# Another table for the attention unit of a four-layer kernel: three shared maxima in place of four, other value phases, GpSimd's jobs at other steps, one store of the maxima

## The chip, the cores and the metric

The kernel runs on one core of a Trainium2 chip. The metric is the device time of one execution in microseconds (us); a time is the median of several runs. The engines are named as in the profile: PE is the matrix engine, PEld its loads of weights, DVE the vector engine, ACT the scalar engine, POOL is GpSimd, SP issues DMAs. A "q" behind an engine's name is its queue.

## What is computed

Four attention layers with residuals on x of 2048 tokens by 576, 32 heads of 18 elements, all in float32: A, B, A, B. Layer A has a key and a value for each head, layer B one key and one value for all heads.

```python
def _A_ref(x, wqkv, wo):
    ...
    q, k, v = qkv[0], qkv[1], qkv[2]
    scores = jnp.einsum("bhqd,bhkd->bhqk", q, k) * (Dh ** -0.5)
    p = _softmax(scores, axis=-1)
    o = jnp.einsum("bhqk,bhkd->bhqd", p, v)
    return (lambda x, *d: x.transpose(*d))(o, 0, 2, 1, 3).reshape(B, S, D) @ wo
...
x = A_x
x = x + _A_ref(_layernorm(x, axis=-1), A_wqkv, A_wo)
x = x + _B_ref(_layernorm(x, axis=-1), B_wq, B_wk, B_wv, B_wo)
x = x + _A_ref(_layernorm(x, axis=-1), A_wqkv, A_wo)
x = x + _B_ref(_layernorm(x, axis=-1), B_wq, B_wk, B_wv, B_wo)
```

## The kernel before

**Work of a layer.** After layernorm and the projections, the heads are taken in 16 pairs; of a pair, head half a = 0 lies on partitions 0 to 63 and a = 1 on 64 to 127, so that a tile of either half uses half of PE's rows. For each pair p and each block u of 512 queries there are three kinds of PE work:

- *m tiles* (lines 590 and 601): scores of 128 queries against 512 keys, 32 tiles for one (p, u). DVE takes each row's maximum (line 606, into `mx`). The maxima are needed as rows of the q operand of the next kind, so they run LEAD = 14 steps ahead of it.
- *e tiles* (line 823): scores of 128 keys against 512 queries with the maxima already subtracted, 32 for one (p, u). ACT takes the exponential (line 827, into a buffer `pt`).
- *value columns* (line 865): `pt` times the values, summed over all keys in the bank `oacc`. They run PV_LAG = 928 columns behind.

Some m tiles are of kind r (line 590): the tile is a difference of two key blocks' scores. ACT takes its relu (line 599) into one buffer named `relu`, which all of them share; some tiles later DVE adds that buffer to the other block's scores and takes the row maximum in one fused instruction (line 604, with a short read of the accumulator behind it). So one DVE instruction serves two tiles, and this is what "shared maximum" means.

**Order.** It is written out by hand in the table UNIT and repeats with a period of 10 phases, called a unit here: 32 m and r tiles, 32 e tiles and 4096 value columns. A phase is a list of tiles and then a number of value columns. A tile is written as kind, head half, rank: `r10` is an r tile of half 1 with rank 0. A step is 4 e tiles, and a unit is 8 steps. Each engine executes its instructions in program order.

**Banks.** m and e tiles share seven PSUM banks. They are kept in a list by last use; a tile with rank 0 takes the bank that was used longest ago, with rank 1 the one after that, and so on. Before PE may write a bank, the ACT or DVE instruction that reads its earlier tile must be done. This is the loop, and the choice of a bank:

```python
def oldest(rank=0):
    return lambda name: bank(lru[rank], name)
...
rows, cols = UNIT[phase % len(UNIT)]
run_todo(LEAD + sum(e_next) / 4)
for kind, a, rank in rows:
    if kind == "e":
        exp_next(a, rank)
    elif m_done[0] < 4 * ns:
        max_mm(oldest(rank))
...
pv_cols(cols - skip)
```

**Jobs at steps.** What is not in the table is given a step with `at` and is emitted by `run_todo` at the start of the first phase that reaches it. For a block (p, u): two POOL instructions turn the maxima into `hl` (`max_final`, lines 797 to 801, emitted two m tiles after the block's last); at NM_AT DVE transposes them and SP stores them to `m_d` (`max_store`, lines 806 and 808); at ROW_AT SP loads them as rows of q (`max_rows`, line 812); at SUM_AT and later steps POOL and SP do the sums, the reciprocals and the output (`o_sum`, `l_part`, `l_inv`, `l_out`, `l_rows`, `o_mul`, `o_out`). Weights of `wo` and of the next layer come in chunks c = 0 to 4 during the attention: SP loads a chunk into `raw` (`load_wsm`, `load_a`, `load_b`; lines 192 to 195), and `finish_loads` lets POOL split it into a high and a low part (lines 176 and 205).

Of the kernel before, what the change touches and what calls it, by code (L numbers as in the profile page):

```python
# [8 lines left out]
F32 = mybir.dt.float32  # L9
# [9 lines left out]
P = 128  # L19
NCH = S // P  # L20
NPAIR = H // 2
# [24 lines left out]
STEPS = 8  # L46
LEAD = 14
NM_AT = 2.5
ROW_AT = 5
SUM_AT = 3  # L50
L_AT = 5
INV_AT = 8
R_AT = 8
# [8 lines left out]

UNIT = [("e00 m10 m02 e10 e01 e10 m00", 448),
# [9 lines left out]
UNIT = [([(o[0], int(o[1]), int(o[2])) for o in rows.split()], cols) for rows, cols in UNIT]  # L75
PV_LAG = 928
UNIT_M = [(kind, a) for rows, _ in UNIT for kind, a, _ in rows if kind != "e"]
assert len(UNIT_M) == 32 and sum(cols for _, cols in UNIT) == 4096


@with_exitstack
def tile_kernel(ctx: ExitStack, tc: tile.TileContext, A_x, A_wqkv, A_wo, B_x, B_wq, B_wk, B_wv, B_wo, out):
    nc = tc.nc
# [6 lines left out]
    dram = ctx.enter_context(tc.tile_pool(name="dram", bufs=1, space=DRAM))  # L90
# [42 lines left out]
    kd_d = dram.tile([2 * DH, 3, 512], F32, name="kd_d")  # L133


    m_d = [dram.tile([2, 2, 4, P], F32, name=f"m_d{i}") for i in range(4)]
    o_d = dram.tile([D, S], F32, name="o_d")
    r_d = dram.tile([H, S], F32, name="r_d")

# [271 lines left out]
    for layer in range(4):  # L411
        is_a = layer % 2 == 0
# [79 lines left out]
        def q_slot(p):  # L492
            return (3, 5, 1)[p % 3] if is_a else (3, 4, 0)[p % 3]
# [173 lines left out]
        def max_pairs():  # L667

            if is_a:
                run_todo(m_done[0] // 4)  # L670
            elif m_done[0] == 44:
                max_store(0, 0)
            elif m_done[0] == 48:
                max_rows(0, 0)
            for i in range(4):
                max_mm(etile if i == 3 else mtile)
            while m_full:
                max_final(*m_full.pop()[0])
# [124 lines left out]
        def max_store(p, u):  # L803

            tr = pool.tile([P, 32], F32, name="tr")
            nc.vector.transpose(tr, nms.pop((p, u)).bitcast(F32))
            for b in range(4):
                nc.sync.dma_start(m_d[u].rearrange("j a q (b i) -> b (j a q) i", b=4)[b], tr[32 * b:32 * b + 16, :])

        def max_rows(p, u):  # L810
            for a in range(2):
                nc.sync.dma_start(big_f[64 * a + KM:64 * a + KE, q_slot(p), u * 512:(u + 1) * 512],
                                  m_d[u][:, a].rearrange("j q p -> j (q p)"))

        def exp_mm(p, u, i, rank):

# [97 lines left out]
        relu, raw = (pool.tile([P, 640], F32, tag="xh", bufs=2, name=n) for n in ("relu", "raw"))  # L914
        todo = {}

        def at(b, f, *args):
            todo.setdefault(b, []).append((f, args))

        for p in range(NPAIR):  # L920
            for u in range(4):
                b = STEPS * (4 * p + u) + STEPS - 1
                if is_a or p or u:
                    at(b + NM_AT, max_store, p, u)
                    at(b + ROW_AT, max_rows, p, u)
                for d, f in ((SUM_AT, o_sum), (L_AT, l_part), (INV_AT, l_inv), (R_AT, l_out), (RB_AT, l_rows),
                             (MUL_AT, o_mul), (O_AT, o_out)):
                    at(b + LEAD + d, f, p, u)
            if p + 1 < NPAIR and is_a:
                for d, f in ((0, diff_in), (3, diff_split), (5, diff_out), (10 if p else 8, diff_rows)):  # L930
                    at(max(LEAD, 32 * p - 8) + d, f, p + 1)
            if is_a and p in (0, 1):
                at(LEAD + 20 + 32 * p, load_rows, q_slot(p + 1), 2 * (p + 1) * DH, DH, 1536, S)
            if p + 1 < NPAIR:
                for i in range(4 if is_a else 2):
                    at(LEAD + 32 * (p - 1) + 1 + 8 * i if p else LEAD + 1 + 4 * i, load_part, p + 1, i)
        for c in range(5):
            at(49 + 4 * c, finish_loads)
            at(48 + 4 * c, load_wsm, c, A_wo if is_a else B_wo, nc.gpsimd, nc.gpsimd, False,
               (raw[:, :288], raw[:, 288:]))  # L940
            if layer < 3:
                b = LEAD + 32 * (NPAIR - 1) + 2 * c
                load = load_b if is_a else load_a
                at(b - 29, finish_loads)
                at(b + 3, finish_loads)
                at(b - 30, load, c, (2,), nc.gpsimd, nc.gpsimd, raw)
                at(b + 2, load, c, (0,), nc.gpsimd, nc.gpsimd, raw)

        def run_todo(st):
            for n in sorted(n for n in todo if n <= st):  # L950
                for f, args in todo.pop(n):
                    f(*args)

        b = LEAD + ns
# [19 lines left out]
        while m_done[0] < 4 * ns:  # L974
            rows, cols = UNIT[phase % len(UNIT)]
            run_todo(LEAD + sum(e_next) / 4)
# [56 lines left out]
```

## Time and profile before

| | |
|---|---|
| median of 3 runs | 5553.27 us (5551.57 to 5559.15) |
| the profiled execution | 5554.74 us |
| its span, first to last instruction | 5553.0 us |
| ACT exponentials, L827 | 8192, busy 4182.4 us |
| DVE row maxima, L606 | 6208, busy 3959.1 us |
| DVE fused maxima, L604 | 992, busy 686.1 us |
| ACT relus, L599 | 992, busy 622.2 us |

The page gives each engine's busy time and its share of the span, then the chain of work that ended last, then groups of instructions by line with their number and mean length. Busy times of ACT and DVE count from an instruction's start to its end, and instructions that follow each other closely overlap by some tenths of a us; how fast an engine really goes is read from the distance of starts in the timeline.

### The profile page before, as it was taken

How to read it: one execution, taken by the hardware profiler on the slowest of the kernel's cores; microseconds unless marked ns; L12 is line 12 of the kernel's file. 1: busy time of each engine (PE TensorE's matmuls, PEld its weight loads, DVE VectorE, ACT ScalarE, POOL GpSimd, SP SyncE). 2: the span in 40 equal slices, each digit the busy share in tenths (PEclk: the TensorE clock that was granted, in tenths of full speed). 3: DMA queues.
4: the chain of work that ended last, by engine and by line, in shares of the span. 5: the costliest groups of instructions: out<-in, count | busy, mean ns of one | idle time of the engine just before them, and what ended most of it. 6: DMA issues, size and time to landing. Idle time of an engine off the chain costs nothing.

```text
span 5553.0 us, 143953 instructions
## 1 busy us (share of the span) xinstructions
PE 5519.8 (99%) x55774; PEld 3110.0 (56%) x55774; DVE 4949.8 (89%) x9489; ACT 4883.1 (88%) x9872; POOL 1836.8 (33%) x2396
## 2 busy tenths in 40 slices
PE   9999999999999999999999999999999999999999
PEld 8655555554855555555686555555548555555556
DVE  4699999998699999999647999999977999999995
ACT  2599999999389999999725999999992999999996
POOL 3143333334233333333412433333342333333332
PEclk9999999999999999999999999999999999999999
DMA  6421111111421101001243211111114211110102
GB/s 199 133 55 47 43 47 42 47 44 24 132 70 24 24 21 24 21 23 25 61 168 111 59 44 46 43 46 45 42 31 137 59 24 24 24 24 21 24 14 81
DMA packets 275188, 301.69 MB, mean 54 GB/s; under 512 B 135246, under 2 KB 193190, under 8 KB 265214
## 3 DMA queue, kind: packets, MB, share of 16 engines
q1 hardware_dynamic: 274502, 292.49, 19.0%
q8 instruction: 437, 7.16, 0.6%
q14 instruction: 249, 2.04, 0.1%
HBM read 168.50 MB, written 119.86 MB: 52 GB/s over the span
## 4 chain that ended last, share of the span: by engine, by line
PE 96%; POOL 1%; issue 1%; DMA 1%; DVE 0%; SPq 0%; ACT 0%; POOLq 0%; ACTq 0%; DVEq 0%
PE oacc L865 37%; PE pse L823 27%; PE psm L601 17%; PE psn L259 7%; PE psq L433 5%; PE psm L590 3%; PE ps L251 0%; DMA big<-qk_d 0%; POOL ev L445 0%; ACT pt L827 0%; DVE mx L606 0%; DMA xo<-in_A_x_dram 0%; DMA raw<-in_B_wk_dram 0%; DMA xx<-qk_d 0%; DMA big<-m_d 0%
## 5 line engine op out<-in xcount | busy, mean ns | idle before, releaser
L827 ACT ACTIVATE pt<-pse 128x512 f32<-128x512 f32 x8192 | 4182.4, 614 | 23.1 <-PE pse L823 11.7
L606 DVE TENSOR_REDUCE mx<-psm 128x1 f32<-128x512 f32 x6208 | 3959.1, 685 | 119.8 <-PE psm L601 77.2
L823 PE MATMUL pse<-big 64*128 64x512 f32 x8192 | 2288.2, 433 | 3.2 <-DMA big<-m_d 1.9
L601 PE MATMUL psm<-big 62*128 62x512 f32 x7200 | 2194.9, 443 | 7.9 <-DVE mx L604 4.3
L823 PEld LDWEIGHTS pse<-big 64*128 64x128 f32 x8192 | 1177.1, 185 | 1071.6 <-ACT pt L827 742.3
L865 PE MATMUL oacc<-pt,vbuf 128*19 128x32 f32 (+11 forms) x26544 | 1731.6, 368 | 4.0 <-DVE oc L176 4.0
L601 PEld LDWEIGHTS psm<-big 62*128 62x128 f32 x7200 | 913.1, 184 | 172.7 <-ACT pt L827 33.9
L865 PEld LDWEIGHTS oacc<-pt,vbuf 128*19 128x19 f32 x26544 | 534.6, 98 | 826.2 <-issue 664.4
L176 POOL TENSOR_SCALAR os<-oc 32x512 f32<-32x512 f32 x512 | 313.2, 612 | 1917.2 <-ACT oc L874 1508.9
L893 POOL TENSOR_TENSOR rl<-lt,mone 128x8 f32<-128x8 f32 x256 | 423.1, 1653 | 984.4 <-DMA lt<-os 933.5
L604 DVE CUSTOM_DVE_ANT_0 relu<-psm,relu 128x512 f32<-128x512 f32 x992 | 686.1, 692 | 32.6 <-PE pse L823 1.1
L599 ACT ACTIVATE relu<-psm 128x512 f32<-128x512 f32 x992 | 622.2, 627 | 0.2
L865 PE MATMUL oacc<-pt,vy 128*19 128x288 f32 (+3 forms) x8176 | 567.2, 383 | 0.0
L441 ACT ACTIVATE ev<-psq 128x512 fp32r<-128x512 f32 (+1 forms) x112 | 66.9, 598 | 327.7 <-PE psq L433 226.2
L906 POOL TENSOR_TENSOR os<-os,rb 96x512 f32<-96x512 f32 x256 | 327.7, 1280 | 26.4 <-DMA rb<-r_d 25.3
L884 POOL TENSOR_TENSOR os<-os,oc 96x512 f32<-96x512 f32 x256 | 327.9, 1281 | 21.3
L865 PEld LDWEIGHTS oacc<-pt,vy 128*19 128x19 f32 x8176 | 190.2, 98 | 239.5 <-issue 196.0
L259 PE MATMUL psn<-wsm,xx 128*128 128x288 f32 x2240 | 307.9, 296 | 0.7 <-ACT pt L827 0.7
L259 PEld LDWEIGHTS psn<-wsm,xx 128*128 128x128 f32 x2240 | 298.6, 188 | 13.7 <-issue 11.7
L447 DVE TENSOR_TENSOR ev<-psq,ev 128x512 fp32r<-128x512 f32 (+1 forms) x84 | 58.0, 691 | 214.1 <-ACT ev L441 195.1
L590 PE MATMUL psm<-big 54*128 54x512 f32 x512 | 215.1, 420 | 0.0
L590 PE MATMUL psm<-xx,big 54*128 54x512 f32 x480 | 201.2, 419 | 0.0
(93 smaller groups left out, 2368.3 us busy)
## 6 DMA issues: line engine op xcount, KB each, us to landing
big<-qk_d SPq DMA_DIRECT2D x172, 432.0 KB
qk_d<-ev SPq DMA_DIRECT2D x96, 512.0 KB
qk_d<-ev SPq DMA_DIRECT2D x120, 256.0 KB
rb<-r_d SPq DMA_DIRECT2D x512, 36.0 KB
o_d<-os SPq DMA_DIRECT2D x512, 36.0 KB
m_d<-tr SPq DMA_DIRECT2D x1024, 2.0 KB
o<-o_d SPq DMA_DIRECT2D x64, 256.0 KB
xx<-qk_d SPq DMA_DIRECT2D x120, 72.0 KB
```

The costliest lines, as they stand in the source:

```text
L259: nc.tensor.matmul(ps, lhs[:, xc, :], wsm[:, wc, h * 288:(h + 1) * 288], start=i == 0, stop=i == len(TERMS) - 1)
L590: nc.tensor.matmul(ps.rearrange("p (h t) -> p h t", h=2) if p == 0 or not is_a else ps, q[b:b + 3 * DH, c0:c0 + P], k, start=True, stop=True)
L599: nc.scalar.activation(t, ps, AF.Relu)
L601: nc.tensor.matmul(ps, q[b:b + KM, c0:c0 + P], k[b:b + KM, kb * 512:(kb + 1) * 512], start=True, stop=True)
L604: nc.vector.tensor_tensor_reduce(t, ps, t, 1.0, LOWEST, OP.add, OP.max, mx[:, r:r + 1])
L606: nc.vector.reduce_max(mx[:, r:r + 1], ps, axis=AX.X)
L823: nc.tensor.matmul(e, k[r:r + KE, kc * P:(kc + 1) * P], q[r:r + KE, u * 512:(u + 1) * 512], start=True, stop=True)
L827: nc.scalar.activation(pt, e, AF.Exp, scale=SCALE)
L865: nc.tensor.matmul(oacc[j:j + DH + 1, cs], v_of(kc)[:, 2 * p + a if is_a else 0, :], pts[p, u, i][:, cs], start=kc < 2 and c0 == 0, stop=k ...
L884: nc.gpsimd.tensor_tensor(t[:96], t[:96], oc[:96], op=OP.add)
L893: nc.gpsimd.tensor_tensor(rl, lts.pop((p, u)), mone, op=OP.pow)
L906: nc.gpsimd.tensor_tensor(t[:96], t[:96], rb[:96], op=OP.mult)
```

## The change

The table UNIT is replaced. Four r tiles a unit become three, so one more of the 32 tiles goes to DVE alone. The phases hold 6 or 7 tiles (before 4 to 7) and 352 to 480 value columns (before 256 to 480). SUM_AT moves `o_sum` by 0.75 of a step. The loads of `wo` move by 2 steps. The loads of the next layer's weights come 4 steps apart (before 2 steps) and each is finished one step after it was started. The transposed maxima are stored with one DMA of all 128 partitions to a larger `m_d` (before four DMAs of 16 partitions each); `max_rows` reads the same values.

```diff
-SUM_AT = 3
+SUM_AT = 3.75
...
-        ("e10 e01 r10 m00", 256),
...
-        ("m10 e00 m12 m00 e11 e01 e10", 448),
-        ("e01 m10 e02 e10 r01 m11 m00", 416),
...
+        ("m00 e10 e01 m10 m11 r00", 448),
+        ("e00 m10 e00 m01 e10 m01 e10", 416),
...
-    m_d = [dram.tile([2, 2, 4, P], F32, name=f"m_d{i}") for i in range(4)]
+    m_d = [dram.tile([4, 2, 4, P], F32, name=f"m_d{i}") for i in range(4)]
...
-            for b in range(4):
-                nc.sync.dma_start(m_d[u].rearrange("j a q (b i) -> b (j a q) i", b=4)[b], tr[32 * b:32 * b + 16, :])
+            nc.sync.dma_start(m_d[u].rearrange("j a q (b i) -> b (j a q) i", b=4), tr)
...
-                                  m_d[u][:, a].rearrange("j q p -> j (q p)"))
+                                  m_d[u][:2, a].rearrange("j q p -> j (q p)"))
...
-            at(49 + 4 * c, finish_loads)
-            at(48 + 4 * c, load_wsm, c, A_wo if is_a else B_wo, nc.gpsimd, nc.gpsimd, False,
+            at(51 + 4 * c, finish_loads)
+            at(50 + 4 * c, load_wsm, c, A_wo if is_a else B_wo, nc.gpsimd, nc.gpsimd, False,
...
-                b = LEAD + 32 * (NPAIR - 1) + 2 * c
+                b = STEPS * 4 * (NPAIR - 1) + 4 * c - 14
...
-                at(b - 29, finish_loads)
-                at(b + 3, finish_loads)
-                at(b - 30, load, c, (2,), nc.gpsimd, nc.gpsimd, raw)
-                at(b + 2, load, c, (0,), nc.gpsimd, nc.gpsimd, raw)
+                at(b + 1, finish_loads)
+                at(b + 33, finish_loads)
+                at(b, load, c, (2,), nc.gpsimd, nc.gpsimd, raw)
+                at(b + 32, load, c, (0,), nc.gpsimd, nc.gpsimd, raw)
```

One line fewer stands ahead of `max_rows`, so lines behind it have a number smaller by one in the changed kernel: the exponential is L826 there, the e tile L822, the value columns L864.

**First place: ACT and DVE, in the middle of a unit.** ACT in the kernel before, from the r tile of the fourth phase on (in brackets the engines or DMA queues whose signal an instruction waits for):

```order
L599 ACTIVATE relu<-psm 128x512 [waits DVE_49,PE_49]
L827 ACTIVATE pt<-pse 128x512 [waits PE_49] x2
L599 ACTIVATE relu<-psm 128x512 [waits PE_49,Activation_49]
L827 ACTIVATE pt<-pse 128x512 [waits PE_49] x7
L599 ACTIVATE relu<-psm 128x512 [waits DVE_49,PE_49]
```

And in the changed kernel, from the r tile of the fifth phase on:

```order
L599 ACTIVATE relu<-psm 128x512 [waits DVE_49,PE_49]
L826 ACTIVATE pt<-pse 128x512 [waits PE_49] x3
L599 ACTIVATE relu<-psm 128x512 [waits DVE_49,PE_49]
L826 ACTIVATE pt<-pse 128x512 [waits PE_49,Activation_49]
L826 ACTIVATE pt<-pse 128x512 [waits PE_49] x7
```

DVE from the transpose at the start of the sixth phase on, before (the two rows of line 604, called ISA here, are the fused maximum and the read of its accumulator):

```order
L806 STREAM_TRANSPOSE tr<-hl_115 128x32 [waits DMAHW2_49,DMAHW1_49,DMAHW7_49,DMAHW0_49,Pool_49]
L604 ISA relu,mx_89<-psm,relu 128x512 [waits PE_49,Activation_49]
L604 ISA mx_89 128x1
L606 TENSOR_REDUCE mx_89<-psm 128x1 [waits PE_49] x2
L604 ISA relu,mx_89<-psm,relu 128x512 [waits PE_49]
```

And in the changed kernel:

```order
L806 STREAM_TRANSPOSE tr<-hl_114 128x32 [waits DMAHW4_49,Pool_49]
L606 TENSOR_REDUCE mx_90<-psm 128x1 [waits PE_49] x2
L604 ISA relu,mx_90<-psm,relu 128x512 [waits PE_49,Activation_49]
L604 ISA mx_90 128x1
L606 TENSOR_REDUCE mx_90<-psm 128x1 [waits PE_49] x3
```

In the changed kernel the sixth phase's tiles for DVE are m00, m10 and m11, and m11 is served by the fused instruction, which reads the relu of r12 (fifth phase). The signal of DVE that the relu of r00 waits for is the one of this fused instruction. In the kernel before, the relu of r01 (seventh phase) waits for the fused instruction of that phase's m10, its first tile for DVE.

**Second place: PE, end of the sixth phase and the seventh.** The changed kernel from m11 on (rows of L601, L590: m and r tiles; L822: e tiles; L864: value columns):

```order
L601 MATMUL psm<-big 128x512 [waits DVE_49]
L590 MATMUL psm<-big 128x512 [waits Activation_49]
L864 MATMUL oacc<-pt,vbuf 19x384 x4
L864 MATMUL oacc<-pt,vbuf 19x64 [waits Activation_49]
L864 MATMUL oacc<-pt,vbuf 19x64 x3
L822 MATMUL pse<-big 128x512
L601 MATMUL psm<-big 128x512 [waits DVE_49]
L822 MATMUL pse<-big 128x512
L601 MATMUL psm<-big 128x512 [waits DVE_49]
L822 MATMUL pse<-big 128x512 [waits Activation_49]
L601 MATMUL psm<-big 128x512 [waits Activation_49]
L822 MATMUL pse<-big 128x512 [waits DVE_49]
```

The kernel before, its sixth phase's value columns and its seventh phase:

```order
L865 MATMUL oacc<-pt,vbuf 19x448 x4
L823 MATMUL pse<-big 128x512 [waits Activation_49]
L601 MATMUL psm<-big 128x512 [waits DVE_49]
L823 MATMUL pse<-big 128x512 [waits Activation_49]
L823 MATMUL pse<-big 128x512 [waits DVE_49]
L590 MATMUL psm<-xx,big 128x512 [waits Activation_49]
L601 MATMUL psm<-big 128x512 [waits Activation_49]
L601 MATMUL psm<-big 128x512 [waits DVE_49]
L865 MATMUL oacc<-pt,vbuf 19x32 x4
```

In the changed kernel the L601 row that waits for ACT, the seventh phase's second m01, is the tile that takes the bank of r00; the last row's e10 takes the bank of m11.

**Third place: POOL, at the load of the next layer's weights near the end of layer 0.** Before (raw is the loaded chunk, os the sums, hl the maxima):

```order
L188 MEMSET raw 128x256
L176 TENSOR_SCALAR big<-raw 128x2x128
L205 TENSOR_TENSOR big<-raw,big 128x2x128
L176 TENSOR_SCALAR os_112<-oc 32x512 x2
L884 TENSOR_TENSOR os_112<-os_112,oc 96x512
L188 MEMSET raw 128x256
L176 TENSOR_SCALAR hl_114<-neg 128x8
L801 TENSOR_TENSOR hl_114<-neg,hl_114 128x8
```

And in the changed kernel:

```order
L188 MEMSET raw 128x256
L176 TENSOR_SCALAR big<-raw 128x2x128
L205 TENSOR_TENSOR big<-raw,big 128x2x128
L176 TENSOR_SCALAR hl_115<-neg 128x8
L801 TENSOR_TENSOR hl_115<-neg,hl_115 128x8
L176 TENSOR_SCALAR os_113<-oc 32x512 x2
L883 TENSOR_TENSOR os_113<-os_113,oc 96x512
L905 TENSOR_TENSOR os_112<-os_112,rb 96x512
```

The two instructions of `hl` stood behind `o_sum` and now stand ahead of it.

More of the change, by code (lines that the diff above doesn't have):

```diff
@@ L60 @@
 TAIL = 2
-UNIT = [("e00 m10 m02 e10 e01 e10 m00", 448),
[9 rows of a table removed]
+UNIT = [("m10 e00 e00 m10 m01 e10", 448),
[9 rows of a table added]
 UNIT = [([(o[0], int(o[1]), int(o[2])) for o in rows.split()], cols) for rows, cols in UNIT]
```

13 rows, old and new, of the table UNIT are left out of this document.

## The prediction

> **What bounds the kernel now.** The page's first and fourth parts come first: which engine is busy, and which engine the chain that ended last runs through.
>
> ```profile
> span 5553.0 us, 143953 instructions
> PE 5519.8 (99%) x55774; PEld 3110.0 (56%) x55774; DVE 4949.8 (89%) x9489; ACT 4883.1 (88%) x9872; POOL 1836.8 (33%) x2396
> ...
> PE 96%; POOL 1%; issue 1%; DMA 1%; DVE 0%; SPq 0%; ACT 0%; POOLq 0%; ACTq 0%; DVEq 0%
> ```
>
> PE is the path, and ACT and DVE stand a little below it. The view by stretches says how regular this is: layer 0 from its second unit on, and one unit (ten phases) of layer 1.
>
> ```profile
> 239.80:1231.50 991.70, 991.70 (x10804) 509.94 (x10801) 965.70 (x1837) 990.51 (x1999) 368.54 (x469) 1.00 0.19 49
> 2010.50:2028.86 18.36, 18.36 (x206) 9.47 (x202) 17.87 (x35) 18.34 (x39) 5.75 (x7) 1.00 0.09 22
> ```
>
> The first row holds 54 units, 991.70 / 54 = 18.36 us each, PE busy throughout. So a unit costs what PE's instructions take, and other engines cost nothing until one keeps PE waiting. I therefore price PE's phases from the timeline of PE (start, length, line; only the starts are used).
>
> ```profile
> 2002.64 0.50 PE L823 MATMUL pse<-big 64*128 64x512 f32 x1
> ...
> 2002.98 0.40 PE L823 MATMUL pse<-big 64*128 64x512 f32 x2
> 2003.21 0.40 PE L590 MATMUL psm<-big 54*128 54x512 f32 x1
> ...
> 2010.47 0.50 PE L823 MATMUL pse<-big 64*128 64x512 f32 x1
> ...
> 2011.28 0.40 PE L601 MATMUL psm<-big 62*128 62x512 f32 x1
> 2011.60 0.95 PE L865 MATMUL oacc<-pt,vbuf 128*19 128x416 f32 x16
> 2012.49 0.50 PE L601 MATMUL psm<-big 62*128 62x512 f32 x1
> ...
> 2013.41 1.00 PE L865 MATMUL oacc<-pt,vbuf 128*19 128x480 f32 x8
> 2014.34 0.49 PE L823 MATMUL pse<-big 64*128 64x512 f32 x1
> ...
> 2015.25 0.73 PE L865 MATMUL oacc<-pt,vbuf 128*19 128x320 f32 x8
> 2015.91 0.50 PE L823 MATMUL pse<-big 64*128 64x512 f32 x2
> ...
> 2016.59 0.63 PE L865 MATMUL oacc<-pt,vbuf 128*19 128x192 f32 x16
> 2017.15 0.50 PE L601 MATMUL psm<-big 62*128 62x512 f32 x2
> ```
>
> A score tile of head half 0 and one of half 1 start together, so tiles cost by pairs. Seven tiles (four slots) take 2010.47 to 2011.60 = 1.13 us; six take 0.92 (2012.49 to 2013.41) or 0.91; four take 0.68. Value columns: the phases with six tiles and 480 and 320 columns last 1.85 and 1.57, so 0.28 / 160 = 1.75 ns a column. The first pair of a phase holds PE 0.34 (2002.64 to 2002.98), the next 0.23: weights that could not be loaded ahead cost 0.11.
>
> **The table: what it removes.** The old phases hold 7, 6, 6, 4, 6, 7, 7, 7, 7, 7 tiles, the new ones six times 6 and four times 7: the four becomes six (+0.23) and two sevens become sixes (-0.22 each), together -0.2 us a unit. Columns are 4096 in both, cut into 17 pieces in both (cumulative columns behind the lag of 928, cut at each 512), so value work costs the same. Where each phase waits for nothing, a unit would take 18.16.
>
> **The table: what it adds.** An r tile goes to ACT (relu) and lets one DVE instruction serve two tiles. Four become three: ACT loses one instruction a unit, DVE gets one more. DVE's and ACT's rows, same stretch:
>
> ```profile
> 2001.14 0.20 DVE L806 STREAM_TRANSPOSE tr<-hl 128x32 f32<-128x32 f32 x1
> 2001.29 0.69 DVE L604 CUSTOM_DVE_ANT_0 relu<-psm,relu 128x512 f32<-128x512 f32 x1
> 2001.90 0.08 DVE L604 DVE_READ_ACCUMULATOR2_ANT mx<- 128x1 f32 x1
> 2001.90 1.28 DVE L606 TENSOR_REDUCE mx<-psm 128x1 f32<-128x512 f32 x2
> ...
> 2013.02 0.69 DVE L604 CUSTOM_DVE_ANT_0 relu<-psm,relu 128x512 f32<-128x512 f32 x1
> ```
> ```profile
> 2000.58 0.61 ACT L599 ACTIVATE relu<-psm 128x512 f32<-128x512 f32 x1
> 2001.21 3.54 ACT L827 ACTIVATE pt<-pse 128x512 f32<-128x512 f32 x7
> ```
>
> Reduces in a row start 0.60 apart (two in 1.28, the last 0.68), so DVE needs 26 x 0.60 + 3 x 0.70 = 17.7, with the transpose 17.9: under 18.16, but closer than before. ACT needs (3.54 - 0.61) / 6 = 0.49 a piece, 36 x 0.49 = 17.6. As rates, both still fit under PE.
>
> As an order they do not. All relus write one buffer. In the new table the second relu (r00, last of the sixth phase) stands right behind the DVE instruction that reads the first one (m11, the tile just ahead of r00), as the rows of ACT and DVE in the section on the change show: ACT cannot start r00 before DVE has finished m11, and DVE has two other tiles of that phase ahead of m11. And the seventh phase's sixth tile, m01, is to take a bank from ACT: with rank 1 it skips the oldest bank (m11's, seven tiles back) and takes r00's, six tiles back. Counted from the first matmul of phase six:
> - DVE starts on its tile 0.53 later (matmul 2012.49, DVE 2013.02);
> - two reduces, 1.20: m11 begins at 1.73;
> - m11 takes 0.61 + 0.08 (2001.29 to 2001.90, then the accumulator): 2.42;
> - hand-over to ACT. No row shows DVE releasing a relu; the nearest is the other way, relu end 2000.58 + 0.61 = 2001.19, DVE start 2001.29: 0.10, so 2.52;
> - relu 0.61: 3.13; release of PE 0.06 (accumulator 4044.74 + 0.08, matmul 4044.88 in the rows further below): 3.19.
>
> PE arrives earlier: phase six lasts 1.85 - 32 x 0.00175 = 1.79, and the fourth slot of a seven-tile phase comes at 0.81 (2010.47 to 2011.28), so at 2.60. The **wait is 0.59**, and m01's weights come late with it, 0.11: 0.70 a unit. Behind m01 on PE stand e10 and the phase's eight value matmuls, and nothing passes: the stall at 4044.88 below holds all that follows too. ACT and DVE then have 0.7 us of relief, so I count no second wait. Bounds for the 0.70: 0.40 (weights ready, hand-over near zero), 1.00 (the transpose, 0.20, in front of the phase's first reduce, and 0.10 more for the hand-overs). A unit becomes 18.36 - 0.20 + 0.70 = **18.86**.
>
> **GpSimd's jobs.** Three stretches of before leave the 18.36:
>
> ```profile
> 1268.20:1290.10 21.90, 19.30 (x202) 9.55 (x201) 17.75 (x34) 18.81 (x38) 10.59 (x17) 1.00 0.13 26
> 2672.70:2692.80 20.10, 19.22 (x203) 9.54 (x201) 17.73 (x35) 18.71 (x39) 11.22 (x15) 1.00 0.16 42
> 4032.30:4056.20 23.90, 21.75 (x202) 10.57 (x201) 17.90 (x34) 18.70 (x38) 10.39 (x17) 0.86 0.11 22
> ```
> ```profile
> 4039.33 0.41 POOL L176 TENSOR_SCALAR big<-raw 128x256 fp32r<-128x256 f32 x1 [3.03 <-DMA raw<-in_B_wk_dram]
> 4040.64 1.28 POOL L176 TENSOR_SCALAR os<-oc 32x512 f32<-32x512 f32 x2
> ...
> 4043.50 0.19 POOL L176 TENSOR_SCALAR hl<-neg 128x8 fp32r<-128x8 f32 x1
> ```
> ```profile
> 4044.01 0.21 DVE L806 STREAM_TRANSPOSE tr<-hl 128x32 f32<-128x32 f32 x1 [3.20 <-POOL hl L801]
> 4044.14 0.68 DVE L604 CUSTOM_DVE_ANT_0 relu<-psm,relu 128x512 f32<-128x512 f32 x1
> 4044.74 0.08 DVE L604 DVE_READ_ACCUMULATOR2_ANT mx<- 128x1 f32 x1
> ```
> ```profile
> 4044.88 0.79 PE L601 MATMUL psm<-big 62*128 62x512 f32 x1 [2.15 <-DVE mx L604]
> ```
>
> The next layer's weights come at a pace of 2 steps, POOL works off a load, then o_sum's three instructions, and hl last; DVE's transpose waits 3.20 for hl and PE 2.15 for DVE. The excess is 3.5 + 1.7 + 5.5 = 10.7 us. The new pace of 4 steps puts one load where two or three stood, and hl now stands ahead of o_sum: I take all of it, **-11**, bounds -11 and 0. What is late next there is the maxima's way through SP behind the six loads of the last chunk; the maxima are due a unit later, so it is covered. The weights of wo 2 steps later and o_sum one phase later lie beside a POOL that is busy 5.75 of 18.36: nothing.
>
> In the last of these stretches the clock is 0.86, and 0.14 x 23.9 = 3.3 us of the 5.5 are that. The Trainium skill ("TensorE: Matmul & The Clock Gate", What's actually happening) says that the clock halves after at least one idle window of about 3.4 us. This trace differs: PE stood 2.15 us in all there. By the rule the new waits of 0.6 never halve the clock; by the rows a wait of 2.15 did once.
>
> **One store of the maxima.** SP spends 1.69 us on four issues and would spend about 0.42 on one:
>
> ```profile
> 2001.37 1.69 SPq L808 DMA_DIRECT2D m_d<-tr  x4
> ```
> ```profile
> PE pse L823 <- DMA big<-m_d: 1.9, 3, 1.2
> ```
>
> PE has waited for maxima 1.9 us in the whole run, so this is worth between -1.9 and nothing; the store is covered by the phases between it and its reader. I take 0.
>
> **The sum.** The profiled execution took 5554.7 (span 5553.0), 1.5 over the median 5553.3. Of the units, 248 have r tiles: before's page counts 992 relus, four each. 248 x (18.86 - 18.36) = +124; loads -11: 5554.7 + 113 = 5667.7, as a median **5666 us**. With 0.40 and 1.00 for the wait: +50 - 11 and +198, so 5592 to 5751.
>
> **Rivals.**
> - *Faster: the wait never reaches PE.* It decides at one point: r00's relu must begin by 2.60 - 0.06 - 0.61 = 1.93 us after phase six starts, 0.6 earlier than I count. For it:
>
> ```profile
> L599 ACTq EVENT_SEMAPHORE  x740: 17/17/17, 228.5 to 5449.4; - x185
> L599 ACT ACTIVATE relu<-psm 128x512 f32<-128x512 f32 x992 | 622.2, 627 | 0.2
> ```
>
>   740 of before's 992 relus already have a separate wait, and ACT stood 0.2 us in all ahead of them. Against it: those stood behind a long ACT queue, or their DVE work was first in its phase; here it is third. The time: 248 x (18.16 - 18.36) = -50, loads -11: 5492. 11 in 100.
> - *Flat.* The wait comes to about 0.25 and just gives back the 0.2 and the loads: 3 in 100.
> - *Slower still: other waits open.* My layout leaves some banks hardly any margin (phase six's m11 behind phase five's last reduce, phase ten's last tile behind r10's relu). Two waits of 0.3 more are 248 x 0.6 = 149: about 5815. 8 in 100.
> - *The clock halves at each wait:* 248 x 3.3 = 818, about 6480. The 21.90 stretch speaks against it: PE stood 2.6 us and the clock stayed 1.00. 1 in 100.
>
> **How the numbers follow.** The forecast's own range (5592 to 5751) holds 77 in 100, a little more with its neighbours; faster by over 0.2% (11 us, what a measurement can tell from no change) 0.11, within 0.03, slower 0.86. The range is 5595 to 5750.
>
> **What would show it.** Right: units of about 18.9 with one gap in PE's rows each, ahead of an L601 tile in the phase after r00, put down to ACT's relu; ACT idle ahead of its second relu for about 0.5 to 1 us a unit, released by DVE; no stretch of the layers' ends above its neighbours. Wrong: units of 18.16 and no relu among what PE waits for; or long units whose gap stands elsewhere. If ACT waits for DVE as I say but PE does not, the bank count is wrong; if the units are longer while clock rows fall below 1.00, the last rival holds.

## The result, and the profile after

The changed kernel takes **5726.32 us** (median of 5 runs, 5725.34 to 5728.34), the kernel before 5554.13 us (5 runs, 5551.57 to 5559.15): a ratio of 1.0308, 95% interval [1.0297, 1.0319]. It is slower by 172 us; 113 were forecast. The profiled execution took 5725.34 us.

The page of the changed kernel: span, busy time, the chain that ended last, and two of the costliest groups (busy time, mean ns of one, then the idle time of the engine ahead of them and who ended it).

```profile
span 5723.6 us, 143368 instructions
...
PE 5606.4 (98%) x55774; PEld 3067.1 (54%) x55774; DVE 5026.7 (88%) x9489; ACT 4831.2 (84%) x9624; POOL 1842.7 (32%) x2396
...
PE 85%; DVE 8%; ACT 3%; issue 2%; POOL 1%; DMA 0%; SPq 0%; ACTq 0%; POOLq 0%; DVEq 0%
...
L601 PE MATMUL psm<-big 62*128 62x512 f32 x7448 | 2461.4, 430 | 91.5 <-ACT relu L599 88.8
...
L599 ACT ACTIVATE relu<-psm 128x512 f32<-128x512 f32 x744 | 452.1, 608 | 140.8 <-DVE mx L604 135.2
```

Before, the chain ran through PE for 96% of the span and DVE had 0% of it; now DVE has 8% and ACT 3%. The tiles of L601 waited 88.8 us for relus, and ACT, which had waited 0.2 us in all ahead of its relus, now waited 140.8, nearly all for line 604 on DVE. The tiles of L601 before, with no relu among what they waited for:

```profile
L601 PE MATMUL psm<-big 62*128 62x512 f32 x7200 | 2194.9, 443 | 7.9 <-DVE mx L604 4.3
```

The view of PE's waits gives the number of times (total, times, longest):

```profile
PE psm L601 <- ACT relu L599: 88.8, 244, 0.7
```

There are 248 units with r tiles: it is one wait a unit. The views by stretches show 40 units of layer 1, first of the kernel before, then of the changed one, where the ends of layers 0 to 2 follow (one unit each, the one that was longest before).

```profile
1735.05:2470.18 735.13, 735.10 (x8004) 377.82 (x8001) 714.82 (x1361) 733.96 (x1482) 230.02 (x280) 1.00 0.10 23
```
```profile
1783.06:2547.89 764.83, 750.26 (x8003) 371.92 (x8001) 727.11 (x1361) 725.94 (x1441) 231.55 (x280) 1.00 0.09 23
...
1311.73:1330.84 19.11, 18.77 (x202) 9.23 (x203) 18.17 (x35) 18.15 (x37) 8.55 (x13) 1.00 0.11 24
2684.40:2703.50 19.10, 18.75 (x208) 9.23 (x200) 18.18 (x35) 18.14 (x37) 8.80 (x11) 1.00 0.12 32
4160.80:4179.90 19.10, 18.75 (x204) 9.22 (x200) 18.18 (x36) 18.13 (x37) 9.46 (x15) 1.00 0.12 25
```

A unit went from 735.13 / 40 = 18.38 us to 764.83 / 40 = 19.12, and PE stands still in it. At the layers' ends a unit is no longer than elsewhere, and the clock is 1.00 throughout. (Below, a unit is the median: 18.37 before and 19.11 after.)

Now the place, in the timelines of PE, DVE and ACT around one seventh phase. It begins at 2003.33; the sixth began at 2001.47.

```profile
2001.47 0.50 PE L601 MATMUL psm<-big 62*128 62x512 f32 x1
...
2003.33 0.50 PE L822 MATMUL pse<-big 64*128 64x512 f32 x1
...
2003.90 0.40 PE L601 MATMUL psm<-big 62*128 62x512 f32 x1
2004.65 0.50 PE L601 MATMUL psm<-big 62*128 62x512 f32 x1 [0.36 <-ACT relu L599]
```
```profile
2002.01 1.29 DVE L606 TENSOR_REDUCE mx<-psm 128x1 f32<-128x512 f32 x2
2003.22 0.68 DVE L604 CUSTOM_DVE_ANT_0 relu<-psm,relu 128x512 f32<-128x512 f32 x1
2003.82 0.08 DVE L604 DVE_READ_ACCUMULATOR2_ANT mx<- 128x1 f32 x1
```
```profile
2001.84 1.60 ACT L826 ACTIVATE pt<-pse 128x512 f32<-128x512 f32 x3
2004.00 0.60 ACT L599 ACTIVATE relu<-psm 128x512 f32<-128x512 f32 x1 [0.56 <-DVE mx L604]
2004.49 5.58 ACT L826 ACTIVATE pt<-pse 128x512 f32<-128x512 f32 x11
2009.95 0.62 ACT L599 ACTIVATE relu<-psm 128x512 f32<-128x512 f32 x1
```

Read it as a chain: two reduces of DVE from 2002.01, the fused maximum that reads the old relu from 2003.22, its accumulator until 2003.90, ACT's next relu at 2004.00, done at 2004.60, PE's tile at 2004.65. ACT stood idle for 0.56 us, and PE's previous tile had started 0.75 us earlier. The list has 88.8 / 244 = 0.36 a wait, less than PE lost, since PE counts as busy until the end of the previous tile (2003.90 + 0.40).

The phases' tile parts (from the first tile to the first value matmul, medians over the 40 units, from the starts of PE's rows) show what else is longer. Without a wait, six tiles take 0.90 to 0.92 us and seven 1.13.

| phase | 1 | 2 | 3 | 4 | 5 | 6 | 7 | 8 | 9 | 10 |
|---|---|---|---|---|---|---|---|---|---|---|
| tiles | 6 | 6 | 6 | 6 | 6 | 6 | 7 | 7 | 7 | 7 |
| us | 0.90 | 0.90 | 0.90 | **1.03** | 0.90 | **0.97** | **1.76** | 1.14 | 1.13 | **1.32** |

Phase seven is 0.63 too long, but phases four, six and ten are together 0.37 too long as well. These gaps are too short for the list of waits. In phase ten and in phase four of the same unit PE's rows show them so, and PEld's row has the load of weights for phase ten's last tile:

```profile
1998.05 0.50 PE L822 MATMUL pse<-big 64*128 64x512 f32 x1
...
1998.62 0.53 PE L822 MATMUL pse<-big 64*128 64x512 f32 x2
1999.08 0.79 PE L864 MATMUL oacc<-pt,vbuf 128*19 128x96 f32 x16
...
2009.73 0.50 PE L601 MATMUL psm<-big 62*128 62x512 f32 x1
...
2010.54 0.57 PE L822 MATMUL pse<-big 64*128 64x512 f32 x2
2011.04 0.85 PE L864 MATMUL oacc<-pt,vbuf 128*19 128x288 f32 x16
```
```profile
2010.62 0.18 PEld L822 LDWEIGHTS pse<-big 64*128 64x128 f32 x1
```

Phase ten's last e tile (the second of the row at 2010.54) starts at 2010.62, just after the relu of ACT from 2009.95 to 2010.57 in the rows above: its bank is that relu's. Its weights load at 2010.62 too, not ahead of it. It costs 0.08 of waiting and about 0.11 for the weights: 2011.04 - 2009.73 = 1.31. Phase four's last e tile (e01, the second of the row at 1998.62) is the same in small: by the table its bank is that of the third phase's last e tile, whose exponential ends at 1998.60; weights and tile start at 1998.65, and the phase is 0.12 too long (1.025 against 0.904 before rounding). In phase six it is r00, in the bank of r12: r12's relu ends at 2001.96, r00's weights load only at 2002.02, and the phase is 0.07 too long.

### The profile page after: what moved, and what is told of

It reads as the page before. It is cut to its first block, busy times and chain, and to the rows that moved or that the text cites. A ratio compares the mean times of both kernels' runs of the same rounds, so it can differ in the third digit from the quotient of the medians.

```text
span 5723.6 us, 143368 instructions
## 1 busy us (share of the span) xinstructions
PE 5606.4 (98%) x55774; PEld 3067.1 (54%) x55774; DVE 5026.7 (88%) x9489; ACT 4831.2 (84%) x9624; POOL 1842.7 (32%) x2396
## 4 chain that ended last, share of the span: by engine, by line
PE 85%; DVE 8%; ACT 3%; issue 2%; POOL 1%; DMA 0%; SPq 0%; ACTq 0%; POOLq 0%; DVEq 0%
PE oacc L864 33%; PE psm L601 21%; PE pse L822 19%; PE psn L259 6%; DVE mx L606 5%; PE psq L433 5%; ACT relu L599 3%; DVE relu L604 3%; PE psm L590 1%; ACT pt L826 0%; POOL ev L445 0%; PE ps L251 0%; DMA big<-qk_d 0%; POOL wsm L205 0%; PE oacc L252 0%
## 5 line engine op out<-in xcount | busy, mean ns | idle before, releaser
L826 ACT ACTIVATE pt<-pse 128x512 f32<-128x512 f32 x8192 | 4233.6, 620 | 104.8 <-PE pse L822 86.0
L606 DVE TENSOR_REDUCE mx<-psm 128x1 f32<-128x512 f32 x6704 | 4183.3, 684 | 81.6 <-PE pse L822 49.0
L601 PE MATMUL psm<-big 62*128 62x512 f32 x7448 | 2461.4, 430 | 91.5 <-ACT relu L599 88.8
L822 PE MATMUL pse<-big 64*128 64x512 f32 x8192 | 2537.5, 442 | 1.7 <-ACT evr L444 1.6
L864 PE MATMUL oacc<-pt,vbuf 128*19 128x416 f32 (+9 forms) x26544 | 1733.0, 368 | 4.6 <-DVE oc L176 4.0
L822 PEld LDWEIGHTS pse<-big 64*128 64x128 f32 x8192 | 1214.0, 184 | 796.8 <-DVE mx L606 370.6
L601 PEld LDWEIGHTS psm<-big 62*128 62x128 f32 x7448 | 1178.7, 185 | 687.2 <-ACT pt L826 251.9
L864 PEld LDWEIGHTS oacc<-pt,vbuf 128*19 128x19 f32 x26544 | 546.4, 97 | 792.4 <-issue 551.9
L604 DVE CUSTOM_DVE_ANT_0 relu<-psm,relu 128x512 f32<-128x512 f32 x744 | 509.4, 685 | 175.7 <-ACT pt L826 173.6
L599 ACT ACTIVATE relu<-psm 128x512 f32<-128x512 f32 x744 | 452.1, 608 | 140.8 <-DVE mx L604 135.2
L864 PE MATMUL oacc<-pt,vy 128*19 128x384 f32 (+3 forms) x8176 | 570.1, 383 | 0.0
L864 PEld LDWEIGHTS oacc<-pt,vy 128*19 128x19 f32 x8176 | 177.9, 98 | 229.4 <-issue 196.6
L433 PE MATMUL psq<-yx,big 128*128 128x512 f32 (+2 forms) x826 | 197.1, 391 | 4.2 <-ACT yx L243 2.2
```

What stands on the lines that cost most here:

```text
L433: nc.tensor.matmul(ps[:n].rearrange("p (u t) -> p u t", u=2)[:, us], w[:, wc, :n], xts[T][:, us, xc, :], start=(xc, wc) == TERMS[0], stop= ...
L599: nc.scalar.activation(t, ps, AF.Relu)
L601: nc.tensor.matmul(ps, q[b:b + KM, c0:c0 + P], k[b:b + KM, kb * 512:(kb + 1) * 512], start=True, stop=True)
L604: nc.vector.tensor_tensor_reduce(t, ps, t, 1.0, LOWEST, OP.add, OP.max, mx[:, r:r + 1])
L606: nc.vector.reduce_max(mx[:, r:r + 1], ps, axis=AX.X)
L822: nc.tensor.matmul(e, k[r:r + KE, kc * P:(kc + 1) * P], q[r:r + KE, u * 512:(u + 1) * 512], start=True, stop=True)
```

## The experiments

Kernels that were measured together share the runs of the kernel before, and each ratio is to those.

### Which part of the change is it

**Table alone** (the kernel before with the new UNIT and nothing else).

```diff
-UNIT = [("e00 m10 m02 e10 e01 e10 m00", 448),
...
+UNIT = [("m10 e00 e00 m10 m01 e10", 448),
...
+        ("m00 e10 e01 m10 m11 r00", 448),
+        ("e00 m10 e00 m01 e10 m01 e10", 416),
...
```

> The kernel before with the new table alone (old steps of GpSimd's jobs, old four stores, SUM_AT 3). Theory (the table's second relu waits for DVE and PE for that relu): the whole loss is the table's, units of 19.1 us, and the load stalls of before (10.7 us) stay: 5726 + 10 = 5735. Rival (the moved jobs or the one store cost time): clearly below 5726, near 5640 if they share the loss.

Measured: 5733.39 us, ratio 1.0318 [1.0304, 1.0332], unit 19.11. The view of PE's waits:

```profile
PE psm L601 <- ACT relu L599: 89.9, 244, 0.8
```

The whole loss is the table's; GpSimd's jobs and the store are worth about 7 us in its company (5733.4 against 5726.3), but the intervals of the two ratios overlap.

**Jobs and store** (the changed kernel with the old UNIT), and **jobs alone** (the old table and four stores).

```diff
-UNIT = [("m10 e00 e00 m10 m01 e10", 448),
...
+UNIT = [("e00 m10 m02 e10 e01 e10 m00", 448),
...
```

> The changed kernel with the old table: only GpSimd's jobs, SUM_AT and the one store are new. Theory: units stay at 18.36, the three stretches of 21.9, 20.1 and 23.9 us fall to 18.4: 5554 - 11 = 5543. Rival (the one store or the later loads cost time): 5554 or more.

```diff
-SUM_AT = 3
+SUM_AT = 3.75
...
-                b = LEAD + 32 * (NPAIR - 1) + 2 * c
+                b = STEPS * 4 * (NPAIR - 1) + 4 * c - 14
...
```

> The kernel before with GpSimd's jobs at the new steps alone: old table, old four stores. Theory: the one store is worth nothing, so this is as the run with jobs and store, 5546. Rival: the store brings the gain, then 5554.

Measured: 5545.57 us, ratio 0.998 [0.9971, 0.9989], and 5549.92 us, ratio 0.9988 [0.9979, 0.9998]. Both gain, as expected; the intervals overlap, so what the one store is worth stays open. (PE waits for the maxima's DMA 8.0 us in seven times with four stores and 4.2 in two with one, but the execution profiled with four stores took 5556.06, 6 us above its median, so this doesn't decide it.) The layers' ends are now as long as their neighbours (third row below), but some of the gain is lost again: in layer 0 (and likewise in layer 2) two early units, where the loads of wo now fall, are longer than 18.37 (first two rows: PE stands in the first, and the clock is 0.91 in the one behind it), and a wait for the maxima's DMA is listed. Stretches, then PE's waits, of the kernel with jobs and store:

```profile
327.37:348.38 21.01, 19.14 (x204) 9.64 (x202) 17.76 (x35) 18.58 (x39) 8.22 (x13) 1.00 0.32 91
348.38:368.26 19.88, 19.88 (x204) 9.74 (x200) 17.86 (x35) 18.61 (x37) 9.48 (x13) 0.91 0.15 34
1268.15:1286.52 18.37, 18.37 (x204) 9.45 (x201) 17.89 (x35) 18.34 (x39) 8.56 (x13) 1.00 0.12 25
```
```profile
PE pse L822 <- DMA big<-m_d: 4.2, 2, 2.4
```

The old table with the new jobs and store is a version that beats both kernels, the one before by 0.2%.

### Is it the one relu buffer

**Two relus** (a second buffer, which takes the place of the 14th exponential buffer; relus alternate).

```diff
-                t = relus[p, u, a, qc] = relu[:, :512]
+                relu_n[0] += 1
+                t = relus[p, u, a, qc] = (relu[:, :512], relu2)[relu_n[0] % 2]
...
-            if len(ring) < 14:
+            if len(ring) < 13:
...
+        relu2 = ptile("relub")
```

> The changed kernel with two relu buffers that take turns (the second in place of one of the 14 buffers of exponentials), so that r00's relu need not wait for m11's maximum. Theory: the 0.63 us that PE waits for the relu in each unit goes; if the 0.1 to 0.2 us gaps in phases 4, 6 and 10 stay, units are 18.5 and the time 5726 - 248 x 0.63 = 5570; if those gaps were ACT's backlog behind the late relu, units are 18.1 to 18.2 and the time about 5490. Rival (DVE with one more instruction a unit is the bound, or the bank order itself): units stay above 18.9, time above 5680.

Measured: 5574.77 us, ratio 1.0032 [1.0019, 1.0045], unit 18.48. The wait for relus is in the list no more; phase seven is back at 1.13 and phase six at 0.91. So the one buffer costs 0.64 us a unit (19.112 - 18.476 before rounding), some 150 of the 172 us. The buffer of exponentials that is missing costs nothing here: in 40 units of layer 1 ACT waits for score tiles alone, never for the value columns that free such a buffer. But phases four (1.02) and ten (1.32) stay long and phase eight becomes 1.19: these gaps are not after-effects of the late relu.

**Swap** (r00 changes places with the seventh phase's first e00, so that it comes later).

```diff
-        ("m00 e10 e01 m10 m11 r00", 448),
-        ("e00 m10 e00 m01 e10 m01 e10", 416),
+        ("m00 e10 e01 m10 m11 e00", 448),
+        ("r00 m10 e00 m01 e10 m01 e10", 416),
```

> The changed kernel with r00 (end of phase 6) and the first e00 of phase 7 in each other's place, nothing else. Theory: the relu then comes when DVE has done m11, PE's wait goes, and the gap of phase 10 with it if it was ACT's backlog: units of 18.2 to 18.5, 5500 to 5570. Rival (DVE's rate or the bank order): units above 18.9, over 5680.

Measured: 5605.06 us, ratio 1.0088 [1.0075, 1.0102], unit 18.62. Phase seven is free (1.13), so the wait can be removed by order alone; but phase eight takes 1.27, with four, six and ten as before. The time is 35 us above the upper end of what I had expected, since the swap opens a gap a phase later.

**Short maxima** (the changed kernel, one buffer; the plain row maxima read 448 of the 512 columns, so an eighth of the keys is left out of them). It asks whether DVE's two tiles ahead of the fused maximum set the wait.

```diff
-                    nc.vector.reduce_max(mx[:, r:r + 1], ps, axis=AX.X)
+                    nc.vector.reduce_max(mx[:, r:r + 1], ps[:, :448], axis=AX.X)
```

> The changed kernel, one relu buffer, with VectorE's plain row maxima over 448 of 512 columns (an eighth of the keys is left out of the maxima). Theory: the wait of phase seven is the end of the chain two reduces, the maximum with the relu's tile, the relu; the two reduces are some 0.06 us shorter each, the wait falls from 0.63 to about 0.50 us, the unit from 19.11 to about 18.98 and the time to about 5694 us. Rival (the wait isn't set by VectorE's two tiles ahead): 5726 us, no change.

Measured: 5692.2 us, ratio 1.0245 [1.0229, 1.026], unit 18.98. The group of the maxima, and PE's waits:

```profile
L606 DVE TENSOR_REDUCE mx<-psm 128x1 f32<-128x448 f32 x6704 | 3839.6, 619 | 371.0 <-PE pse L822 178.2 <-PE psm L601 77.0 <-PE psm L590 30.0
```
```profile
PE psm L601 <- ACT relu L599: 58.2, 244, 0.8
```

A reduce went from 684 ns to 619; the wait fell by (88.8 - 58.2) / 244 = 0.125 us, two reduces' 0.065. That fits the chain that I had written down, with two reduces in it. (In this run the profile puts ACT's wait ahead of the relu down to PE. The timeline still has the relu 0.10 behind the accumulator, from 2000.60 to 2000.70, as in the chain above.)

### What are the gaps that stay

The first guess was local: phase four's e01 and phase ten's last e00 come a little early for their banks, and 32 value columns moved ahead of them would cover it. All three runs have two relu buffers.

```diff
-        ("e10 m01 e00 m10 m00 e10", 416),
-        ("e00 m11 m00 m10 e10 e01", 352),
+        ("e10 m01 e00 m10 m00 e10", 448),
+        ("e00 m11 m00 m10 e10 e01", 320),
```

> The kernel with two relu buffers, 32 value columns moved from phase 4 to phase 3 (416, 352 become 448, 320). Theory: phase 4's gap of 0.12 us is its last e tile that comes 0.03 us too early for ACT's exponential behind the evacuation of the sums, and pays 0.1 us for weights loaded late; starting the phase 0.055 us later removes all of it: units of 18.36, 5575 - 29 = 5546. Rival (the gap is ACT's or DVE's rate): it comes back in another phase, units stay near 18.48, 5575.

```diff
-        ("m00 e10 e01 m10 m11 r00", 448),
+        ("m00 e10 e01 m10 m11 r00", 416),
...
-        ("m00 e10 e02 e10 m01 r10 m00", 352),
+        ("m00 e10 e02 e10 m01 r10 m00", 384),
```

> The kernel with two relu buffers, 32 value columns moved from phase 6 to phase 9 (448, 352 become 416, 384). Theory: phase 10's gap of 0.19 us is its last tile waiting for the relu of r10, the last of four ACT instructions of a phase that is shorter (1.85) than these four (1.91); with phase 9 at 1.91 the gap goes: units of 18.29, 5575 - 47 = 5528. Rival: DVE or ACT are bound over the unit and the gap moves: 5575.

The third takes both edits.

> Both moves of columns together. If the gaps are separate accidents of the table, units of 18.17 and 5575 - 76 = 5499, faster than before by 1%. If DVE (17.9 us of work a unit) or ACT is the next bound, part of it comes back: 18.3 and 5530 or more.

Measured: 5571.11 us, ratio 1.0026 [1.0016, 1.0037]; 5561.1 us, ratio 1.0009 [1.0, 1.0018]; 5557.99 us, ratio 1.0001 [0.9992, 1.0011]. The guess fell: units of 18.47, 18.42 and 18.41, where 18.48 was the start. Of phase four's gap 0.05 went, and 0.05 came to phase five; of phase ten's and eight's 0.05 each, and 0.05 came to phase seven. ACT's timeline of the third shows why the gaps mostly only move (from the sixth phase into the next unit):

```profile
1952.17 0.66 ACT L600 ACTIVATE relub<-psm 128x512 f32<-128x512 f32 x1
1952.80 5.58 ACT L827 ACTIVATE pt<-pse 128x512 f32<-128x512 f32 x11
1958.25 0.62 ACT L600 ACTIVATE relu<-psm 128x512 f32<-128x512 f32 x1
1958.73 3.57 ACT L827 ACTIVATE pt<-pse 128x512 f32<-128x512 f32 x7
1962.49 1.58 ACT L827 ACTIVATE pt<-pse 128x512 f32<-128x512 f32 x3 [0.18 <-PE pse L823]
```

For 10 us ACT works without a pause, a piece every 0.49 us ((5.58 - 0.62) / 10 is 0.50, (3.57 - 0.62) / 6 is 0.49); it waits for PE only at the start of the next unit. (A piece shows 0.62, so pieces overlap by some 0.13 us, not by several tenths.) The new table puts 23 of ACT's 36 pieces into phases five to ten: 23 x 0.49 = 11.3 us, in phases that take PE 11.2 us without waits (their length in the last run below). The 0.05 that came to phase seven seems to be DVE's: by the table its last e10 takes the bank of m11, and it starts at 1952.96, 0.06 behind m11's accumulator on DVE (until 1952.90); no run tests this alone. Three runs tell ACT's rate from DVE's, again with two relu buffers:

**Short exponentials** (448 of 512 columns from the 15th to the 1984th exponential of a layer; an eighth of those is left out), **short maxima** (as above) and **both**.

```diff
-            nc.scalar.activation(pt, e, AF.Exp, scale=SCALE)
+            k = 448 if 14 <= sum(e_next) < 1984 else 512
+            nc.scalar.activation(pt[:, :k], e[:, :k], AF.Exp, scale=SCALE)
```

> The kernel of e3_two_relus, with the exponentials from the 15th to the 1984th of a layer taken over 448 of their 512 columns (an eighth of those exponentials is left out; TensorE's work is the same). What stays of the gaps there: a unit of 18.48 us against 18.11 without waits. Theory 'ScalarE's backlog': 26 of ScalarE's 36 operations of a unit fall into phases four to ten, and its exponentials come late for TensorE; each is then about 0.05 us shorter, the gaps of phases four, eight and ten close, the unit is about 18.1 us and the time about 5485 us. Rival 'VectorE's rate' (the maxima hold the banks): the unit stays at 18.48 and the time at 5575 us.

> The kernel of e3_two_relus, with VectorE's plain row maxima taken over 448 of 512 columns (an eighth of the keys is left out of the maxima). Theory 'ScalarE's backlog': nothing of it changes, unit 18.48 us, time 5575 us. Rival 'VectorE's rate': each maximum is about 0.06 us shorter, the gaps close, unit about 18.1 us and time about 5485 us.

> f1_short_exp and f2_short_max in one: two relu buffers, the exponentials from the 15th to the 1984th of a layer and all plain row maxima over 448 of 512 columns (an eighth of each is left out; TensorE's work is the same). With the short exponentials alone phases four, eight and ten were free of gaps, phases one and six had 0.08 us more each, and VectorE was busy for 118.1 of 120 us. Theory: what stayed there is VectorE's rate, the next bound once ScalarE's is off; with both shorter, the unit falls from 18.30 to 18.11 us and the time to about 5486 us. Rival: the two new gaps come from the banks that the two engines leave in another order, whatever VectorE's speed; the unit stays at 18.30 and the time at 5531 us.

Measured: 5530.87 us, ratio 0.9954 [0.9938, 0.9971]; 5571.27 us, ratio 1.0025 [1.0015, 1.0035]; 5490.77 us, ratio 0.988 [0.9863, 0.9896]. The same 40 units of layer 1 (length; PE, PE's weight loads, DVE, ACT, POOL busy) with two relus, then with short exponentials, short maxima, and both:

```profile
1738.80:2478.12 739.32, 739.29 (x8003) 375.09 (x8001) 722.65 (x1361) 725.43 (x1442) 231.72 (x280) 1.00 0.10 23
```
```profile
1729.11:2461.73 732.62, 732.56 (x8002) 350.43 (x8001) 723.13 (x1361) 675.27 (x1441) 232.16 (x280) 1.00 0.10 24
```
```profile
1743.32:2482.46 739.14, 739.14 (x8002) 377.62 (x8000) 671.13 (x1361) 725.18 (x1442) 232.23 (x280) 1.00 0.10 24
```
```profile
1717.82:2444.08 726.26, 726.26 (x8002) 352.80 (x8001) 671.22 (x1361) 675.43 (x1441) 231.85 (x280) 1.00 0.10 24
```

A faster DVE alone changes nothing (its busy time goes from 722.65 to 671.13, the length stays). A faster ACT closes phases four, eight and ten (0.90, 1.14, 1.16), as the theory wanted, but half of the gain expected did not come: phases one and six become 0.08 longer, with DVE busy 723.13 of 732.62. With both shorter these go too, and the unit is 18.15. So the table runs into two limits one right behind the other: ACT's backlog first, then DVE's rate.

The banks say the same. The table's order tells which tile had a bank before, and the traces when its reader was done (medians of the 40 units). With two relus the tiles that hold up phases four, eight and ten are the last e tile of each, all in banks that ACT had read: they start 0.05 us behind two exponentials and r10's relu. With short exponentials the late tiles of phases one and six, e10 and m11, start 0.06 and 0.07 us behind a reduce of DVE.

## Why the prediction was right in kind and short in size

- **Unit without waits, 18.16: right.** With the waits taken off, by a second buffer and shorter work on ACT and DVE, the unit is 18.15. The gain that the table was good for by PE's slots alone, 0.2 us, is real.
- **The wait of the seventh phase, 0.70: right in place, a little too high.** The chain was counted as 3.19 us from phase six's start to PE's release; the rows give 2004.65 - 2001.47 = 3.18. What was off is PE's arrival: phase six, counted as 1.79, lasts 2003.33 - 2001.47 = 1.86, so the phase is 1.76 - 1.13 = 0.63 too long and not 0.70. A second buffer takes 0.64 a unit away, shorter reduces shift it as counted. The rival in which the wait never reaches PE fell.
- **"ACT and DVE then have 0.7 us of relief, so I count no second wait": this is the step that failed**, a term of the sum sized at zero. It was 0.33 us a unit (18.48 with two buffers, 18.15 with the limits off too), 0.33 x 248 = 82 us; about half of it went with shorter exponentials (18.30), the rest only with shorter maxima as well. Two errors lie in it. ACT gets no lasting relief: it stands idle for 0.56 us just there, being the middle of the chain, and then works for 10 us without a pause. And the rates were compared over the whole unit (36 pieces x 0.49 = 17.6 us of 18.16), where the table crowds 23 of them into 11.2 us.
- **The rival "slower still"** had the right kind and one right place, phase ten's last tile behind r10's relu; that gap is 0.19, not 0.3. Its other place, m11 behind phase five's last reduce, was no gap in the changed kernel, where m11 starts 0.2 us after that reduce; it became one only with the short exponentials. Phase four's it did not name. It should have been a term of the forecast.
- **The sum.** 18.15 + 0.64 + 0.33 = 19.12, against 18.16 + 0.70: +0.26 a unit, or 62 to 64 us over 248 units (the three terms add up by construction, each being the step from one run to the next), and the forecast was short by 5726 - 5666 = 60. That 5726 lies inside the stated range is in part luck: the range came from bounds on the wait and on the jobs, and what was missing was a term with no bounds at all.
- **GpSimd's jobs, -11: about right.** 248 x (19.11 - 18.37) is 184 us and the kernel lost 172, so all the rest gives -12; the layers' ends show no stall in the changed kernel. With the old table the jobs and the store give 0.2%, some of it lost again in early units.
- **The store, 0:** not told apart from nothing.
- **The clock:** it stayed 1.00 through 244 waits, as the stretch of before with its clock at 1.00 had said.

## What to carry to other kernels

Where one engine is the path and two others stand within a few per cent below it, a table must be tried against each of them over every stretch between two places where that engine runs dry, not as a mean over the unit: 0.1 us too much there is paid at every unit. A buffer that two steps share makes the order of a third engine's work (here DVE's two other maxima) part of the path; a chain written out from starts in the timeline gives such a wait to a few hundredths. Here the wait did not relieve ACT, which stood idle in its chain and then had its backlog still to do.

## What the runs showed of the hardware that was not expected

A bank that comes 0.04 to 0.08 us late cost PE 0.12 to 0.19: phase four's tile started 0.04 and phase ten's 0.08 after the e tile ahead of it, and the phases were 0.12 and 0.19 longer than those without a wait. In both, PEld loaded the late tile's weights only as the tile started (1998.65, 2010.62). Such gaps are in no list of waits, as PE still counts as busy: the stretch of the kernel with two relus shows PE busy 739.29 of 739.32 us, and yet the same 40 units take 13 us less (739.32 - 726.26) with ACT's and DVE's work shortened.
